# A fused linear-attention and SwiGLU block: all sixteen token tiles in Strassen pairs of the down projection, with the attention quotient inside its contraction

## Chip, cores and metric

One core of one Trainium2 chip. The metric is the device time of one execution in microseconds, the median of several runs. Engines: TensorE (PE) multiplies matrices, VectorE (DVE), ScalarE (ACT) and GpSimd (POOL) work on elements, SyncE (SP) issues transfers.

## The reference

The input x has 2048 tokens of 512 columns, bf16. It is normalised once, and two blocks read the result:

```python
xn = layernorm(x)
# A: linear attention, 32 heads of 16 columns
q, k, v = heads(xn @ wqkv)
pq, pk = phi(q), phi(k)              # phi(t) = (t + 1 if t > 0 else exp(t)) + 1e-6
kv, z = sum_s pk v^T, sum_s pk
o = (pq @ kv) / (pq . z + 1e-6)
# B: SwiGLU, 1792 hidden columns
h = silu(xn @ w_gate) * (xn @ w_up)
out = x + o @ wo + h @ w_down
```

## The kernel before

The kernel writes out its instructions by hand. Each call of `K.add` appends one entry to a list: an engine, its instructions, the keys that it reads (`r`) and writes (`w`), and older contents of the same memory (`a`). `number` turns the dependencies into semaphore waits. Every engine runs its entries in the order in which they were added; SP's transfers too go in that order. Tokens come in 16 tiles of 128.

*Phase one.* An order written out as one string (line 536 on) normalises the tiles, transposes them into `xnT`, and forms q and k (`proj`, L444, 512-column products). phi is made of an exponential on ACT (L465), a minimum on POOL (L472) and a sum on DVE (L483); phi(k) is `pk`, phi(q) is `pq`. `gacc` (L493) collects the products of xn with phi(k) in four PSUM banks, and `z_add` (L510, POOL) sums phi(k) over the tiles.

*Conventional gate and up products.* For the first three token tiles (`T0` = 384 columns), `gu` (L565) and `hop` (L613) make h for each of the 14 blocks of hidden columns. Beside them run the squares and maxima of the weights (L749, L756) for a power-of-two scale, kv (L625), its product M with wo (L711), the sum z over all partitions (L638), the weights' scaling by that power (`scale`, L849 and L850), and the x sums (L857) for the next stage.

*Strassen gate and up products.* The other 13 tiles make gate and up together in a Strassen-Winograd scheme: for each block `fc` and each half `q` of the tokens there are seven products of two 128-row steps (`prod`, L896, 416 columns), where a plain scheme has eight. ACT keeps and copies partial results between banks (`seed` L906, `keep5` L911) and forms silu (`gate0` L921, `gate1` L926); DVE combines PSUM with SBUF (`u4` L931, `up22` L936, `h21` L946); POOL makes the fourth quarter of h (`h22`, L940). DVE also sums the weights for two blocks ahead (`w_sums`, L857). `fill` puts single 512-column products of the down projection of tiles 0 to 3 (`ounits`: 14 of h with wd, L719, and four of the quotient with M, L723) between the Strassen products.

*The attention quotient.* For one tile after the other: POOL multiplies phi(q) by z into `pz` (L665), for six of the tiles folds it once (L674), DVE sums it over each head (`den_sum`, L678) and takes the reciprocal (L684), POOL multiplies phi(q) by that (`pq_mul`, L691), and SP transposes the result into a slot of `pk` (L697). `after` keys on `pq_mul` and `pz_mul` make POOL wait for a named sum of DVE.

*Down projection.* Tiles 4 to 15 go in six pairs through the same seven-product scheme, with seven steps of 128 hidden rows in each half. ACT copies and scales the pair's h (`hcopy`, L1076); DVE forms four sums of its quarters (`h_sum`, L1088, 128 x 896) and of wd's quarters (`t_sum`, L1039; `t1_part`, L1030); `dprod` (L1104) has seven 256-column products; `attn` (L1110) adds the quotient's part with four more products to each of the four outputs; ACT copies two partial results (L1116, L1120), DVE combines (`dkeep_y` L1124 and `du4` L1130, both from PSUM) and adds x (`dout`, L1136), and SP stores (L729).

```python
S_[0] = A21 + A22; S_[1] = S_[0] - A11
S_[2] = A11 - A21; S_[3] = A12 - S_[1]
```

are the four h sums of a pair, A11 and A12 the first and second half of the hidden columns of its first tile, A21 and A22 those of its second.

Of the kernel before, what the change touches and what calls it, by code (L numbers as in the profile page):

```python
# [9 lines left out]
P = 128  # L10
# [19 lines left out]
SX = -22  # L30
# [6 lines left out]
ORDER = tuple(range(14)) + (15, 14)  # L37
SLOT = {t: i for i, t in enumerate(ORDER)}
PAIRS = (4, 6, 8, 10, 12, 14)
H7 = 448  # L40
FOLD = range(3, 9)


class _Program:


# [6 lines left out]
    def add(self, eng, fns, r=(), w=(), dma=False, a=(), own=()):  # L53
# [11 lines left out]
        held = set().union(*[self.readers.get(k, set()) for k in own])  # L65
# [56 lines left out]
def bass_parallel_sum__linear_attn_block__swiglu_ffn__prompt_kernel(nc, A_x, A_wqkv, A_wo, B_x, B_w_gate, B_w_up, B_w_down, out):  # L122
# [5 lines left out]
    with contextlib.ExitStack() as es:  # L128
# [6 lines left out]
        xn = sb("xn", [P, NT, D], bf)  # L135
# [13 lines left out]
        pk = sb("pk", [P, NT, D], bf)  # L149
        pq = sb("pq", [P, NT, D], bf)  # L150
        hT = sb("hT", [P, 2, NFC, 512], bf)
# [12 lines left out]
        out_sb = sb("out_sb", [P, 2, D], bf)  # L164
# [27 lines left out]
        def tsum(ap):  # L192
# [15 lines left out]
        junks = [b_[:, :, :].rearrange("p a b -> p (a b)").bitcast(bf)[:, 0:F // 2] for b_ in (p5, c22)]  # L208
        xs = sb("xs", [P, 2, 2 * H7], f16)
        asd = sb("asd", [P, 8], f32)  # L210
        as1 = sb("as1", [P, 1], f32)
        as1b = sb("as1b", [P, 1], bf)
        sd = sb("sd", [P, 1], f32)
        ed = sb("ed", [P, 2], f32)
        idn = sb("idn", [P, 1], f32)
        sx = sb("sx", [P, 1], f32)
        iso = sb("iso", [P, 1], f32)
        sm = sb("sm", [P, 1], f32)
        psum = E(nc.psum_tensor("pb", [P, 8, 512], f32))
# [236 lines left out]
        def phi_exp(i, t):  # L456
            b = at[i, t]
            buf, bkey = ef[:, b - 4, :], ("ef", b - 4)
            if i == 0 and t in later:
                buf, bkey = pq[:, t, :], ("pq", t)  # L460
# [6 lines left out]
        def phi_min(i, t):  # L467
            buf, bkey = ef[:, at[i, t] - 4, :], ("ef", at[i, t] - 4)
            if i == 0 and t in later:
                buf, bkey = pq[:, t, :], ("pq", t)  # L470
# [5 lines left out]
        def phi_sum(i, t):  # L476
            b = at[i, t]
            dst, dkey = ((pk[:, t, :], ("pk", t)) if i else (pq[:, t, :], ("pq", t)))
            low, lkeys = (flo[:, t:t + 1], [("flo", t)]) if t in CENTRED else (1e-6, [])
            val, mid, keys = banks[b][:, :], ef[:, b - 4, :], [B(b), ("ef", b - 4)]  # L480
            if i == 0 and t in later:
                val, mid, keys = tq[later[t]], pq[:, t, :], [("tq", later[t]), ("pq", t)]
# [47 lines left out]
        def run(text):  # L530
            late = {int(w[1:]) for w in text.split() if w[0] == "z"}
            later.update({t: i for i, t in enumerate(int(w[1:]) for w in text.split() if w[0] == "u" and int(w[1:]) in late)})
            for w in text.split():
                steps[w[0]](int(w[1:]))

        run("""
            S0 M1 a0 b0 c0 R0 d0 F2 C1 S3 e0 N0 W1 r0 K0 o0 f0 R3 w1 S2 K1 P3 k0 S1 R2 J0 W3 x0 k1 Q1 L2 R1 w3
            m0 X2 q1 r1 Z2 Q3 s0 x1 o1 q3 S5 y1 K3 m1 k3 R5 n1 s1 G0 z1 L5 J1 x3 S9 K2 D5 Q0 z3 m3 S4 k2 R9 q0
            y3 P9 s3 G1 x2 S8 R4 m2 D9 Q2 z0 q2 P4 s2 R8 k5 z2 L8 n3 D4 S15 q5 x5 y0 S12 m5 G2 D8 y5 s5 q9 y2
            n5 S10 R15 k9 n0 y9 u5 R12 n9 k4 x9 L15 u9 D15 q4 m9 x4 L12 R10 s9 m4 q8 y4 D12 S11 P10 k8 z8 s4  # L540
            n4 R11 D10 G9 S13 x8 N11 A11 G5 m8 u4 y8 n2 s8 D11 G3 R13 S14 A0 P13 k15 S7 R14 k12 n8 D13 x15 L14
            S6 m15 q10 x12 D14 s15 m12 k10 y10 s12 n10 k11 x10 u10 R7 m10 q15 x11 s10 q11 m11 y15 L7 R6 s11
            D7 n15 k13 y11 u15 q13 n11 x13 L6 u11 D6 m13 q14 y13 s13 n13 q12 y14 u13 n14 k14 y12 u14 n12 q7
            x14 u12 m14 k7 y7 L1 s14 D0 D1 n7 k6 x7 u0 m7 q6 u7 x6 s7 m6 G4 y6 s6 n6 G12 u2 G14 u6 u1 G6 u8 G10
            u3 G11 G15 G8 G13 G7
        """)
# [11 lines left out]
        def gu(j, extra=(), er=(), ew=()):  # L558
            fc = j
            n = (len(extra) + 7) // 8  # L560
            todo = list(extra)
            for b, w_, key in ((gb(j), wg, "wg"), (gb(j) + 1, wu, "wu")):
                fns = []
                for c in range(NDC):
                    fns.append(lambda e, c=c, b=b, w_=w_: e.matmul(  # L565
                        banks[b][:, 0:T0], w_[:, c, fc * P:(fc + 1) * P], xnT[:, c, 0:T0],
# [794 lines left out]
```

## Time and profile before

| what | value |
|---|---|
| median of three runs | 199.56 us (199.41 to 199.59) |
| span of the profiled execution, first to last instruction | 198.2 us |
| what the median lies above that span | 1.4 us |
| TensorE's granted clock | 1.00 throughout |
| stage: Strassen gate and up products | 68.98 to 152.20 us |
| stage: down projection, to PE's end | 152.20 to 196.20 us |

The page gives the profiled execution's span; the time around it is taken from the median of the runs. How to read the profile's lines: in the table of engines, busy time, share of the span, number of instructions. In the groups: line, engine, operation, written and read tensors, shapes, count, then busy time and the mean of one in ns, then idle time of the engine before them and what ended it. In the timelines: start in us, length in us (of a run of several, if "x2" or more), engine, line, operation. In the view of one line: least, median and greatest length in ns. In the stretches: their length, then busy time of PE, weight loads, DVE, ACT, POOL with numbers of instructions, then clock and transfers.

### The profile page before, as it was taken

What the parts mean: (1) busy time and instruction counts of PE and PEld (TensorE: products, weight loads), DVE (VectorE), ACT (ScalarE), POOL (GpSimd) and SP (SyncE); (2) the same over time, 40 slices, a digit from 0 to 9 for tenths busy, and PEclk for the clock granted to TensorE, in tenths of its full rate; (3) what the DMA queues carried; (4) which work ended last, traced back from release to release, by engine and by line L of the source; (5) the groups of instructions that cost most, each with busy time, mean ns of one, the idle gap of its engine ahead of it and who ended that gap; (6) DMA issues with size and microseconds to landing.
All of it is one profiled execution on the core that took longest, in us unless ns stands there. A gap on an engine that the chain in (4) does not pass through costs nothing.

```text
span 198.2 us, 3561 instructions
## 1 busy us (share of the span) xinstructions
PE 193.8 (98%) x1193; PEld 115.2 (58%) x1207; DVE 170.6 (86%) x328; ACT 157.3 (79%) x314; POOL 127.6 (64%) x158
## 2 busy tenths in 40 slices
PE   8899999999999999999999999999999999999995
PEld 2344444444655555555555555555555888888884
DVE  2999998896997799887888998887888999998886
ACT  3799888699698998898999888998897967575300
POOL 3687877799999487689778877868579004413220
PEclk9999999999999999999999999999999999999999
DMA  5943248799900000111110221111000012132223
GB/s 171 360 131 81 61 86 231 211 275 373 348 14 0 3 0 0 28 26 30 28 26 2 55 53 26 26 26 31 2 0 2 3 40 66 33 77 66 45 65 121
DMA packets 28899, 15.97 MB, mean 81 GB/s; under 512 B 17232, under 2 KB 28880, under 8 KB 28880
## 3 DMA queue, kind: packets, MB, share of 16 engines
q1 hardware_dynamic: 28320, 15.28, 28.1%
q10 hardware_dynamic: 560, 0.46, 0.7%
q8 instruction: 9, 0.15, 0.3%
q14 instruction: 10, 0.08, 0.1%
HBM read 9.70 MB, written 2.10 MB: 60 GB/s over the span
## 4 chain that ended last, share of the span: by engine, by line
PE 94%; DVE 2%; DMA 2%; issue 1%; ACT 0%; POOL 0%; SPq 0%
PE pb L896 35%; PE pb L1104 16%; PE pb L444 13%; PE pb L565 9%; PE pb L493 7%; PE pb L719 6%; PE pb L1110 5%; DMA x_sb<-in_A_x_dram 2%; PE pb L723 2%; PE pb L625 0%; PE pb L711 0%; DVE pq L483 0%; PE pb L407 0%; POOL ef L472 0%; DVE stats L307 0%
## 5 line engine op out<-in xcount | busy, mean ns | idle before, releaser
L691 POOL TENSOR_TENSOR pq<-pq,rden 128x512 bf16<-128x512 bf16 x16 | 16.9, 1056 | 36.2 <-DVE rden L684 26.7
L896 PE MATMUL pb<-xnT,wgu 128*128 128x416 bf16 x112 | 26.6, 339 | 0.0
L444 PE MATMUL pb<-wqkv,xnT 128*128 128x512 bf16 x110 | 25.1, 379 | 0.2
L665 POOL TENSOR_TENSOR pz<-pq,zbc 128x512 f32<-128x512 bf16 x16 | 18.9, 1180 | 5.1 <-ACT pz L658 3.5
L565 PE MATMUL pb<-xnT,wgu 128*128 128x384 bf16 x112 | 19.9, 326 | 0.1
L931 DVE TENSOR_TENSOR pb<-p,pb 128x416 f32<-128x416 f32 x28 | 16.6, 595 | 3.6 <-PE pb L896 1.9
L472 POOL TENSOR_SCALAR ef<-ef 128x512 bf16<-128x512 bf16 x25 | 15.5, 620 | 5.8 <-ACT ef L465 5.6
L926 ACT ACTIVATE zacc<-pb,iw 128x416 bf16<-128x416 f32 x28 | 16.4, 614 | 3.1 <-PE pb L896 2.3
L444 PEld LDWEIGHTS pb<-wqkv,xnT 128*128 128x128 bf16 x112 | 10.9, 98 | 13.4 <-DVE pk L483 0.4
L936 DVE TENSOR_TENSOR c<-pb,p 128x416 f32<-128x416 f32 x28 | 16.4, 588 | 2.3 <-PE pb L896 0.3
L465 ACT ACTIVATE ef<-pb 128x512 bf16<-128x512 f32 x25 | 14.8, 593 | 3.9 <-PE pb L444 3.9
L940 POOL TENSOR_TENSOR hT<-c,zacc 128x416 bf16<-128x416 f32 x16 | 15.3, 974 | 2.3 <-ACT zacc L926 1.7
L510 POOL TENSOR_TENSOR zacc<-zacc,pk 128x512 f32<-128x512 f32 x13 | 16.0, 1232 | 1.0
L906 ACT ACTIVATE pb<-pb 128x416 f32<-128x416 f32 x28 | 13.7, 501 | 3.0 <-PE pb L896 1.9
L896 PEld LDWEIGHTS pb<-xnT,wgu 128*128 128x128 bf16 x112 | 10.9, 98 | 8.7
L921 ACT ACTIVATE zacc<-pb,iw 128x416 bf16<-128x416 f32 x28 | 15.7, 626 | 0.0
L565 PEld LDWEIGHTS pb<-xnT,wgu 128*128 128x128 bf16 x112 | 10.8, 98 | 7.0 <-DVE xn L613 0.2
L1104 PE MATMUL pb<-wgu,xnT 128*128 128x256 f16 (+1 forms) x112 | 14.9, 273 | 0.0
L896 PE MATMUL pb<-xnT,wqkv 128*128 128x416 bf16 x56 | 14.4, 339 | 0.3
L896 PE MATMUL pb<-wo,wqkv 128*128 128x416 f16 x56 | 14.4, 339 | 0.0
L896 PE MATMUL pb<-GT,wqkv 128*128 128x416 f16 x56 | 14.4, 339 | 0.0
L307 DVE BATCH_NORM_STATS2 stats<-x_sb 128x6 f32<-128x512 bf16 x16 | 10.8, 678 | 3.2 <-DMA x_sb<-in_A_x_dram 3.2
(202 smaller groups left out, 494.1 us busy)
## 6 DMA issues: line engine op xcount, KB each, us to landing
x_sb<-in_A_x_dram SPq DMA_DIRECT2D x14, 128.0 KB, 3.8
wgu<-in_B_w_gate_dram SPq DMA_DIRECT2D x2, 896.0 KB, 5.2
wgu<-in_B_w_up_dram SPq DMA_DIRECT2D x2, 896.0 KB, 8.0
wd<-in_B_w_down_dram SPq DMA_DIRECT2D x2, 896.0 KB, 13.1
out_dram<-out_sb SPq DMA_DIRECT2D x24, 64.0 KB, 1.6
wqkv<-in_A_wqkv_dram SPq DMA_DIRECT2D x3, 256.0 KB, 4.4
wqkv<-in_A_wqkv_dram SPq DMA_DIRECT2D x1, 512.0 KB, 6.3
wo<-in_A_wo_dram SPq DMA_DIRECT2D x1, 512.0 KB, 8.8
```

The costliest lines, as they stand in the source:

```text
L444: K.add("pe", [(lambda e, c=c: e.matmul(banks[b][:, :], src[:, c, t * P:(t + 1) * P], wqkv[:, c, col:col + D], start=(c == 0), stop=(c == ...
L472: K.add("pool", lambda e: e.tensor_scalar(out=buf, in0=buf, scalar1=top, scalar2=0.0, op0=ALU.min, op1=ALU.max), r=[bkey] + tkeys, w=[bkey])
L510: K.add("pool", lambda e: e.tensor_tensor(out=dst, in0=acc, in1=more, op=ALU.add), r=[key, mkey], w=[dkey])
L565: fns.append(lambda e, c=c, b=b, w_=w_: e.matmul(banks[b][:, 0:T0], w_[:, c, fc * P:(fc + 1) * P], xnT[:, c, 0:T0], start=(c == 0), stop=( ...
L665: K.add("pool", lambda e: e.tensor_tensor(out=halves(i), in0=two(pq[:, t, :]), in1=two(zbc[:, :]), op=ALU.mult), r=[("pq", t), ("zbc",)] + ...
L691: K.add("pool", lambda e: e.tensor_tensor(out=heads(pq[:, t, :]), in0=heads(pq[:, t, :]), in1=rden[:, i, :][:, :, None].broadcast_to([P, N ...
L896: K.add("pe", [(lambda e, c=c: e.matmul(banks[bank][:, 0:TS], L[i][:, c, :], R[i][:, c, ts], start=(start and c == 0), stop=(c == 1), skip ...
L921: K.add("act", lambda e: e.activation(sil4[:, q, :], bk(a), ACT.Silu, scale=iw[:, 0:1]), r=[B(a), ("iw",)], w=[("sil4", q)], a=[("zacc", 0 ...
L926: K.add("act", lambda e: e.activation(sil4[:, 2 + q, :], bk(d), ACT.Silu, scale=iw[:, 0:1]), r=[B(d), ("iw",)], w=[("sil4", 2 + q)], a=[(" ...
L931: K.add("dve", lambda e: e.tensor_tensor(out=bk(d), in0=p5[:, q, :], in1=bk(b), op=ALU.subtract), r=[B(b), ("p5", q)], w=[B(d)])
L936: K.add("dve", lambda e: e.tensor_tensor(out=c22[:, q, :], in0=bk(b), in1=p5[:, q, :], op=ALU.subtract), r=[B(b), ("p5", q)], w=[("c22", q)])
L1104: K.add("pe", [(lambda e, k=k: e.matmul(split(banks[b][:, 0:HD]), L[:, k, :], cut[:, :, k * P:(k + 1) * P], start=(start and k == 0), stop ...
```

## The change

Several things are changed together.

1. **All 16 tiles in pairs.** `PAIRS` has eight pairs of any two tiles. `ounits`, `oout`, `fill` and `attn` go, and with them the 512-column products between the Strassen products.
2. **The quotient inside the contraction.** The transposed quotient of a tile is stored as two more steps beside the seven of each half of h, and M's quarters as two more steps beside wd's. Each of the seven products of a pair has nine steps, each h sum 1152 columns instead of 896, and `tx` adds four sums of M's quarters. The transposition is split in two.
3. **Memory.** One tensor `big` holds h and the quotient, over what were xn, pk and phase one's buffers. phi(q) of tiles 2 to 15 is kept where x lay; x is loaded a second time after the tile's transposition (`xagain`, SP). h no longer is copied: `h21` scales while it writes, and `hscale` scales in place what `h21` doesn't write (tiles 0 to 2 and from half of tile 9 on).
4. **The quotient.** `pq_mul` multiplies pz, which already holds phi(q) z, by the reciprocal; M's rows are divided by z instead (`z_column`, `z_turn`, `m_evac`). The fold goes; the head sums are full width for all tiles.
5. **Engines.** Of the 32 h sums 14 go to POOL and 18 to DVE; of the 21 weight sums four go to POOL; of the weight scalings eight go to DVE, three to ACT and three to POOL; the five maxima on DVE become squares on ACT. `dkeep_y` reads p5 in SBUF instead of PSUM.
6. **Dependencies.** `add` keeps every same-engine dependency except PE's, and orders two engines that read one bank. The `after` keys go.
7. **Order.** Everything from phase one to the end stands in one string; weight loads are spread into phase one. The Strassen products' bank b alternates between blocks.

```diff
-PAIRS = (4, 6, 8, 10, 12, 14)
+PAIRS = ((0, 1), (3, 4), (5, 6), (7, 8), (2, 9), (10, 11), (12, 13), (14, 15))
...
+            if k[0] == "bank":
+                deps |= {d for d in self.readers.get(k, ()) if self.ops[d]["eng"] != eng}
...
-            if o["eng"] == eng and not o["dma"] and d not in held:
-                raw = any(self.last_w.get(k) == d for k in r)
-                if eng == "pe" or not (raw or dma):
-                    continue
+            if o["eng"] == eng == "pe":
+                continue
...
+        pq = _Tiles(stretch(PQ, 2) + [x_sb[:, t, :] for t in range(2, NT)])
+        pk = _Tiles(stretch(7 * S, 8) + stretch(S9 + 7 * S, 8))
...
             K.add("pool", lambda e: e.tensor_tensor(
-                out=heads(pq[:, t, :]), in0=heads(pq[:, t, :]),
-                in1=rden[:, i, :][:, :, None].broadcast_to([P, NH, DH]), op=ALU.mult),
-                r=[("pq", t), ("rden", i)] + list(after), w=[("pq", t)])
+                out=two(pq[:, t, :]), in0=halves(i),
+                in1=rden[:, i, :][:, :, None, None].broadcast_to([P, NH, 2, DH // 2]), op=ALU.mult),
+                r=[("pz", i), ("rden", i)], w=[pqk(t)])
...
         def turn(t):
+            for h in (0, 1):
+                K.add("sp", lambda e, h=h: e.dma_start_transpose(
+                    out=big9[:, h, 7:9, t * P:(t + 1) * P], in_=pq[:, t, h * HD:(h + 1) * HD]),
+                    r=[pqk(t)], w=[("qT", t, h)], ...
...
+            K.add("dve", lambda e: e.scalar_tensor_tensor(
+                out=hslot(fc, lo), in0=bk(b), scalar=sx[:, 0:1], in1=sil4[:, q, :], op0=ALU.mult, op1=ALU.mult),
...
+        def hscale(t, n, half, eng):
+            lo = t * P if t < C0 else max(t * P, T1)
+            v = big9[:, half, 0:7, lo:(t + n) * P]
+            sc, k = (sx[:, 1:2], ("sx1",)) if t < C0 else (sx[:, 0:1], ("sx",))
+            times(eng, v, v, sc, ...)
...
+        def h_sum(p, i, eng="dve"):
...
+            K.add(eng, lambda e: e.tensor_tensor(out=S_[i], in0=a, in1=b, op=op),
...
-        def dprod(p, i, b, start, ks=range(7)):
+        def dprod(p, i, b, start, ks=range(9)):
...
-                out=c22[:, r, 0:HD], in0=dk(d), scalar=iso[:, 0:1], in1=x_sb[:, t, HD:], op0=ALU.mult, op1=ALU.add),
+                out=c22[:, r, 0:HD], in0=p5[:, r, 0:HD], scalar=iso[:, 0:1], in1=x_sb[:, t, HD:], op0=ALU.mult, op1=ALU.add),
...
+        def xagain(t):
+            K.add("sp", lambda e: e.dma_start(x_sb[:, t, :], xin[t * P:(t + 1) * P, :]), w=[("x", t)],
+                  a=[("Sd", 2, i) for i in range(3) if ("x", t) in xo[i]], dma=True)
```

The new order is a string of some 1,120 words. `pr.fc.i.q` is product i of block fc and half q, `dp.p.i` product i of pair p, `hx.p.i.e` h sum i of pair p on engine e (a ACT, v DVE, p POOL), `ws` a weight sum, `sk` a weight scaling, `bc` a copy of a quarter of wd, `ta`, `tm`, `tx` sums of wd's and M's quarters, `hs` an h scaling, `hb` h22, `ha` h21, `uu` u4, `up` up22, `se` seed, `ke` keep5, `pz`, `ds`, `dr`, `pm`, `tr` the quotient's steps, `xr` a second load of x, `dk`, `dy`, `du`, `do` the steps of a pair's outputs, `tb` the load of silu's table (now among pair 5's steps, where it stood ahead of the conventional products, L991). Two pieces, from the end of the Strassen products to the second pair, and the last:

```
tm.2.0 ke.13.1 up.13.0 hx.0.3.v uu.13.1 dp.0.5 pz.13 tx.2 tm.2.1 dp.1.1 pr.13.4.0 tm.3.1 ha.13.0
hb.12.1 bc.21.1.a pr.13.3.1 pm.10 dp.0.6 hx.2.2.p xr.3 de.1 hs.9.1.0.v dk.0 hs.14.1.0.a sj.13.1
hb.13.0 pr.13.7.1 tx.3 up.13.1 dp.1.2 du.0 dp.0.2 pr.13.4.1 xr.4 tm.3.0 dp.0.7 xr.6 hb.13.1
hx.1.0.v hx.1.2.p pz.12 dp.1.5 xr.5 hx.1.1.v dp.1.6 tm.4.1 tx.4 tm.4.0 dp.0.3 dy.0 dk.1 du.1 dp.1.7
...
dp.7.5 dp.6.7 do.5.2 de.7 hx.7.2.p dp.6.3 dy.6 dk.7 dp.7.6 do.6.3 hx.7.3.v do.6.1 dp.6.4 du.7
do.6.2 dy.7 do.6.0 dp.7.3 dp.7.7 do.7.3 dp.7.2 dp.7.4 do.7.1 do.7.0 do.7.2
```

More of the change, by code (lines that the diff above doesn't have):

```diff
@@ L528, in bass_parallel_sum__linear_attn_block__swiglu_ffn__prompt_kernel @@
         }
[L530 to L545, printed above, removed]
@@ new lines, in gu, with gu_kv, gate_conv @@
+                K.add("pe", fns, r=sum([xkeys(t) for t in range(C0)], []) + [(key, fc // 7) for fc in CONV[j]] +
+                      [(key + "c", fc) for fc in CONV[j]] + list(er), w=[B(b)] + list(ew))
+        def gu_kv(j):
+            gu(j, 0, kv_fns(), [("GT", c) for c in range(NDC)] + [("wqkv", 2, 0)], [B(0)])
+        def gate_conv(j):
+            K.add("act", lambda e: e.activation(sil[:, j % 2, 0:TW], banks[gb(j)][:, 0:TW], ACT.Silu),
+                  r=[B(gb(j))], w=[("sil", j % 2)])
@@ L618, in gt_evac, with hjk @@
+        def hjk(fc, lo, n):
+            return [("hj", fc, b) for b in range((lo - T0) // TS, (lo + n - 1 - T0) // TS + 1)]
         def gt_evac(c, eng):
@@ L766, in gather, with top_square @@
+        def top_square(k):
+            tops = [i for i in range(NN) if NORM[k][i][3] == "top"]
+            col = asum[:, NN * k + tops[0]:NN * k + tops[-1] + 1]
+            K.add("act", lambda e: e.activation(col, col, ACT.Square), r=[("asum", k, i) for i in tops], w=[("asum", k, i) for i in tops])
         def gather():
@@ L1326, in bass_parallel_sum__linear_attn_block__swiglu_ffn__prompt_kernel @@
+        """)
+        K.add("sp", [], r=[("out", t, c) for t in range(NT) for c in (0, HD)])
         K.number()
```

881 lines of the change are left out of this document (361 added, 520 removed).

## The prediction

> **What bounds the kernel now.** I read the page's table of engines and its chain first, then the busy time by stage, then the chain in order of time.
>
> ```profile
> span 198.2 us, 3561 instructions
> PE 193.8 (98%) x1193; PEld 115.2 (58%) x1207; DVE 170.6 (86%) x328; ACT 157.3 (79%) x314; POOL 127.6 (64%) x158
> PE 94%; DVE 2%; DMA 2%; issue 1%; ACT 0%; POOL 0%; SPq 0%
> ```
>
> PE is on the chain for 94% of the span and busy for 98%. The busy time by stage (columns: PE, weight loads, DVE, ACT, POOL) shows how near the others are. The four stretches are the end of phase one, the conventional gate and up products (prep), the Strassen gate and up products (U), and the down projection (D):
>
> ```profile
> 40.10:48.74 8.64, 8.59 (x42) 3.91 (x41) 6.82 (x8) 8.54 (x16) 8.07 (x8) 1.00 1.01 322
> 48.74:68.98 20.24, 20.09 (x133) 12.24 (x134) 17.28 (x32) 17.56 (x40) 16.73 (x14) 1.00 0.32 104
> 68.98:152.20 83.22, 82.86 (x455) 44.25 (x460) 72.08 (x137) 76.23 (x147) 64.78 (x65) 1.00 0.10 21
> 152.20:196.20 44.00, 43.88 (x395) 38.13 (x394) 39.64 (x79) 24.03 (x33) 9.68 (x10) 1.00 0.20 53
> ```
>
> In U, DVE works 72.1 and ACT 76.2 of 83.2 us, with POOL at 64.8; in D, POOL is nearly idle. So the bound is PE, but only while its stage stays as long as it is. The chain in order of time prices PE's work, start and length in us:
>
> ```profile
> 144.39 0.65 PE pb L719 x3
> 145.04 3.52 PE pb L896 x20
> ...
> 156.64 3.06 PE pb L1104 x28
> ...
> 160.90 0.44 PE pb L1110 x4
> ...
> 196.17 0.48 DVE out_sb L1136
> ```
>
> A 512-column product costs 0.217 us, a 416-column one 0.176, a 256-column one 0.1093 (L1104) or 0.110 (L1110).
>
> **What the change does to PE.** It removes 4 x 14 products of L719 and 4 x 4 of L723 (72 x 0.217 = 15.6), 6 x 7 x 7 of L1104 (294 x 0.1093 = 32.1) and 12 x 8 of L1110 (96 x 0.110 = 10.6): 58.3 us. It adds 8 pairs x 7 products x 9 steps, 504 x 0.1093 = 55.1, and some 0.2 for the z column. Net: -3.0 us. Against the profiled execution that is 198.2 - 3.0 = 195.2 of span; the median of the runs stands 1.4 above the span, so 196.6 is the time if PE stays the bound. But the 72 removed 512-column products were PE's filler: 83.2 - 14 x 28 x 0.176 = 14.2 us, some 66 of them, ran between the Strassen products of U. U shrinks from 83.2 us to 14 x 28 x 0.176 = 69.0 plus six interleaved down products of 9 x 0.1093, 5.9, and 0.8 of others: 75.7 us. DVE, ACT and POOL have much the same work to do in it.
>
> **What the change does to POOL and DVE.** Two views must be read together: the timelines of DVE and of POOL at the same moment. First, a sum of two SBUF tiles on DVE that starts during a POOL instruction:
>
> ```profile
> 189.15 1.06 POOL L691 TENSOR_TENSOR pq<-pq,rden 128x512 bf16<-128x512 bf16 x1 [3.24 <-DVE rden L684]
> ```
> ```profile
> 189.29 1.40 DVE L1088 TENSOR_TENSOR xnT<-GT 128x896 f16<-128x896 bf16 x1
> ```
> ```profile
> L1088 DVE TENSOR_TENSOR xnT<-GT x3: 609/615/1398, 161.8 to 189.3; 128x896 f16<-128x896 bf16 x3
> ```
>
> It takes 1.40 us for 0.61: POOL ends at 190.21, DVE at 190.69, 0.48 us later. So it waits until POOL is done and then needs 0.48, its 0.61 less 0.13 of start. The other way round, and with an f32 input:
>
> ```profile
> 70.21 1.39 POOL L665 TENSOR_TENSOR pz<-pq,zbc 128x512 f32<-128x512 bf16 x1 [0.85 <-ACT pz L658]
> 71.58 2.98 POOL L850 TENSOR_SCALAR wgu<-wgu,sw 128x1024 bf16<-128x1024 bf16 x2
> ```
> ```profile
> L850 POOL TENSOR_SCALAR wgu<-wgu,sw x3: 1114/1887/1889, 63.6 to 73.4; 128x1024 bf16<-128x1024 bf16 x3
> ```
> ```profile
> L857 DVE TENSOR_TENSOR wqkv<-xnT,GT x1: 1868/1868/1868, 70.6 to 70.6; 128x1664 f16<-128x1664 bf16 x1
> ```
> ```profile
> 41.89 0.68 DVE L483 SCALAR_TENSOR_TENSOR pq<-pb,ef 128x512 bf16<-128x512 f32 x1
> 42.49 0.73 DVE L483 SCALAR_TENSOR_TENSOR pq<-hT,flo,pq 128x512 bf16<-128x512 f32 x1
> 43.16 2.77 DVE L483 SCALAR_TENSOR_TENSOR pq<-hT,pq 128x512 bf16<-128x512 f32 x2
> ```
>
> Here a DVE x sum begins at 70.6 inside POOL's L665, ends late at 72.5, and POOL's scaling of 71.58, behind it, takes 1.89 instead of 1.11. Two DVE sums of two SBUF tiles took 2.77 at 43.16, where one of the same kind took 0.73 at 42.49. DVE instructions that read PSUM show nothing of it (this one ran inside a POOL instruction that began at 163.86 and took 1.06):
>
> ```profile
> 164.54 0.43 DVE L1130 TENSOR_TENSOR pb<-pb,p 128x256 f32<-128x256 f32 x1 [0.28 <-PE pb L1104]
> ```
>
> So POOL's instructions and those of DVE that read only SBUF (two inputs, or one scaled) exclude each other. I call their summed time the **pair's** time; it can't be less than the stage.
>
> [...]
>
> The prices:
>
> ```profile
> L665 POOL TENSOR_TENSOR pz<-pq,zbc 128x512 f32<-128x512 bf16 x16 | 18.9, 1180 | 5.1 <-ACT pz L658 3.5 <-DVE xn L1088 1.6
> L691 POOL TENSOR_TENSOR pq<-pq,rden 128x512 bf16<-128x512 bf16 x16 | 16.9, 1056 | 36.2 <-DVE rden L684 26.7 <-DVE wqkv L857 8.6 <-DVE as L802 0.8
> L940 POOL TENSOR_TENSOR hT<-c,zacc 128x416 bf16<-128x416 f32 x16 | 15.3, 974 | 2.3 <-ACT zacc L926 1.7 <-DVE c L936 0.5
> L1018 POOL TENSOR_SCALAR wgu<-wd,sd 128x896 bf16<-128x896 bf16 x4 | 4.0, 1012 | 3.5 <-DVE mixb L1030 3.5
> L674 POOL TENSOR_TENSOR pz<-pz 128x256 f32<-128x256 f32 x6 | 4.0, 667 | 0.5
> L510 POOL TENSOR_TENSOR zacc<-zacc,pk x13: 1151/1157/1818, 45.5 to 61.3; 128x512 f32<-128x512 f32 x13
> L857 DVE TENSOR_TENSOR wqkv<-wgu x7: 680/680/970, 66.7 to 134.6; 128x1024 f16<-128x1024 bf16 x7
> L857 DVE TENSOR_TENSOR wqkv<-wqkv,wgu x7: 415/417/472, 67.4 to 140.4; 128x512 f16<-128x512 f16 x7
> ```
>
> The order puts 14 of the 32 h sums on POOL, 1152 columns each. No row has that. Two-input POOL instructions run from 667 ns at 256 columns to 1157 at 512, 1.91 ns a column, whatever their types: 0.67 + 896 x 1.91 ns = 2.38 us. The low bound is the one-input L1018: 1.012 x 1152/896 = 1.30; the high one is L940's rate, 2.70. I take 2.38, as L665, L510, L674 and L940 lie on that line and L1018 has one input.
>
> POOL from the end of the projections (40.1) on: 15 z adds and two scalings 19.7; 16 pz 18.9; 16 quotients, now from f32 pz, between 1.06 and 1.18, at 1.1: 17.6; 28 h22 27.3; 14 h sums 33.3; four weight sums 5.4; three weight scalings 3.3; five h scalings 5.1; two wd copies 2.0; half of M 1.1; the last two minima 1.2. Together 134.9; neighbours' records overlap by about 0.04, so 130.5. DVE's SBUF-only instructions, each less 0.13: 18 h sums of 0.61 (0.615 + 256 x 0.51 ns - 0.13; 0.51 is (680 - 417)/512 from L857) 11.0; 17 weight sums 6.5; four x sums 3.5; eight weight scalings now on DVE 2.6; T parts and T sums 5.1; four M sums 1.2; h and wd scalings 1.3; eight dkeep_y, which now read p5 instead of PSUM, 2.8. Together 34.0. The pair needs **164.5 us** after 40.1; before it was 99.3 (the four POOL shares above) + some 25 = 124 of 156. PE has 156.1 - 3.0 = 153.1 there.
>
> The last h sum is followed by four products of 0.98 (3.9 us), the last output sum (0.48) and its store (1.6). So 40.1 + 164.5 + 6.0 + 1.4 outside the span = 212.0 if the pair never idles. In 40.10:48.74, with ready work queued, POOL was busy 93%; at 93% the pair takes 177 and the time is 224.5. I take 98%, nearer full since DVE fills POOL's gaps: 167.9 and, rounded, **215.5 us**.
>
> **Edits costed at nothing, and what covers them.** `add` now keeps every same-engine dependency off PE, and orders readers of a bank on two engines: an added wait costs DVE the 0.08 by which records overlap, only between direct neighbours; below 2 us in all, hidden unless DVE is the bound. What queues behind it on DVE are PSUM sums that PE waits for. Removed hcopies (ACT) and top squares: ACT is not the bound in D. The split transposes and the second loads of x go on SP's queue:
>
> ```profile
> L697 SPq DMA_TRANSPOSE pk<-pq x16: 1189/1196/1197, 78.9 to 190.2; - x16
> x_sb<-in_A_x_dram SPq DMA_DIRECT2D x14, 128.0 KB, 3.8
> out_dram<-out_sb SPq DMA_DIRECT2D x24, 64.0 KB, 1.6
> ```
>
> 32 half transposes at 0.6 to 1.2 us take SP 19 to 38 us of 150 and 14 loads at about 0.5 another 7, so stores are not held up for long. Each x load lands in 3.8 us and is issued eight or more products (7.9 us) ahead of its dkeep_y: hidden, at most 4 us if the last were late. The weight loads move ahead of transposes in phase one; one transpose behind 896 KB could be late by some 4 us, with three projections queued before its reader: nothing. The load of silu's table is written at pair 5 now, though silu is used from the conventional products on:
>
> ```profile
> L991 ACT ACT_TABLE_LOAD x1 | 1.3, 1283 | 0.0
> ```
>
> one more load of 1.3 us on ACT at most, in prep or in D, where ACT has room (17.6 of 20.2 and 24.0 of 44.0): nothing, 1.3 without that cover.
>
> **The rivals.** (a) *PE stays the bound*: the sums fall into POOL's gaps, 196.6, faster. It would need the pair's demand under 153; against it stands 164.5. Even without exclusion U's 75.7 us would be nearly full: DVE's 72.1 loses two x sums and two output adds and gains six weight scalings, full-width head sums and the first h, T and M sums, an estimate of 75; ACT's 76.2 loses ten weight scalings (11.5) and gains the norms and evacuations of M and more of wd's norms and copies, an estimate of 73. (b) *Sums of 16-bit tiles on POOL are cheap*: at 1.30 the pair loses 14 x 1.08 = 15.1, demand 149.4, and near-full DVE and ACT cost a few per cent of U: 199 to 205. For it: no row has two 16-bit inputs of one step. [...] (c) *DVE, in order, becomes the bound*: each of its 35 SBUF-only instructions in U waits on average half a POOL instruction, 0.55, so 19 on top of 75: 94 for 75.7; in D 31 x 0.7 on 39: 61 for 49.5. 196.6 + 18 + 11.5 = 226.
>
> **How the numbers follow.** Forecast 0.58 (207 to 224: 2.16 us per POOL sum and start-ups that overlap, to the pair at 93%); (a) 0.12; (b) 0.13; (c) 0.17. The range reaches from 201, the middle of (b), to 226. What a measurement tells from no change is 0.2%, 0.4 us. Faster: (a) and the luckiest part of (b), 0.13; same 0.02; slower 0.85.
>
> **What would show it.** L1088's successor on POOL at 2.2 to 2.5 us (1.3 speaks for b); DVE's h and weight sums late by hundreds of ns whenever a POOL instruction is under way; PE busy under 93% with the chain passing through POOL and DVE in U and early D; PE idle before products that read a DVE result. PE at 98% and a chain of PE alone would prove the pair wrong; ACT or SPq on the chain would mean a cause that I have not priced.

## The result and the profile after

| | before | after |
|---|---|---|
| median | 199.49 us (199.09 to 199.59) | 235.51 us (234.43 to 236.89) |
| ratio, 95% interval | | 1.182 (1.177 to 1.187) |
| span of the profiled execution | 198.2 us | 232.8 us |

The change costs 36 us, where the forecast said 16. In this table and those below, executions that fell in a second, slower state (one of e2, 231.7 us, and one of e4, 207.8 us) are left out of medians and ranges. The page after, with the table of engines:

```profile
PE 203.8 (88%) x1248; PEld 119.2 (51%) x1253; DVE 195.9 (84%) x341; ACT 145.8 (63%) x288; POOL 177.2 (76%) x172
```

PE no longer fills the span: 29 us of it are idle, where before 4.4 were. The chain that ended last stops after 1% of the span at a wait that the profile does not show, so the stretches have to tell where the time went (PE, weight loads, DVE, ACT, POOL, then the granted clock). They are a part of phase one, U, D to PE's end, and the last part of D:

```profile
30.00:40.00 10.00, 7.95 (x28) 3.10 (x30) 5.04 (x9) 4.36 (x11) 3.83 (x7) 0.83 1.15 319
...
76.93:164.03 87.10, 79.63 (x455) 41.33 (x452) 86.06 (x152) 72.35 (x144) 80.86 (x68) 1.00 0.09 21
164.03:230.52 66.49, 55.29 (x450) 45.77 (x450) 49.11 (x77) 15.21 (x24) 38.58 (x19) 0.92 0.24 64
...
210.00:232.80 22.80, 17.40 (x144) 14.77 (x144) 13.53 (x24) 1.50 (x4) 3.79 (x2) 0.93 0.23 64
```

The same part of phase one before:

```profile
30.00:40.00 10.00, 9.95 (x47) 4.55 (x47) 8.91 (x17) 7.49 (x16) 7.18 (x13) 1.00 0.79 223
```

Three different things show. In phase one every engine works less than before, PE does 28 products for 47, and the DMA share is higher. In U DVE is busy 86.1 of 87.1 us and PE is not. In D no engine is full: something makes them wait for each other.

**Phase one.** The timeline of SP (start, length, line, operation), and PE at the same time:

```profile
25.87 0.58 SPq L247 DMA_DIRECT2D wgu<-in_B_w_gate_dram  x1
26.49 1.19 SPq L443 DMA_TRANSPOSE xnT<-big  x1
27.73 0.58 SPq L247 DMA_DIRECT2D wd<-in_B_w_down_dram  x1
28.36 5.13 SPq L443 DMA_TRANSPOSE xnT<-big  x3
```
```profile
31.96 12.37 PE L464 MATMUL pb<-wqkv,xnT 128*128 128x512 bf16 x47 [2.48 <-DMA xnT<-big]
```

The transposes stand behind large weight loads. From issue to landing they take a median of 3.7 us after, and 2.5 before:

```profile
xnT<-big SPq DMA_TRANSPOSE x14, 3.7
```
```profile
xnT<-xn SPq DMA_TRANSPOSE x14, 2.5
```

**U and early D.** POOL's h sums cost what was forecast, but DVE's sums beside them are late. POOL first, then DVE:

```profile
L1020 POOL TENSOR_TENSOR xnT<-big 128x1152 f16<-128x1152 bf16 x6 | 15.0, 2505 | 6.4 <-PE pb L1038 6.4
```
```profile
156.51 2.54 POOL L1020 TENSOR_TENSOR wqkv<-big 128x1152 f16<-128x1152 bf16 x1
...
163.50 2.74 POOL L1020 TENSOR_TENSOR xnT<-big 128x1152 f16<-128x1152 bf16 x1
...
174.72 2.87 POOL L1020 TENSOR_TENSOR xnT<-big 128x1152 f16<-128x1152 bf16 x1
```
```profile
156.76 2.77 DVE L962 TENSOR_TENSOR wgu<-wgu,mixb 128x896 f16<-128x896 bf16 x1
...
163.95 2.91 DVE L1020 TENSOR_TENSOR xnT<-big 128x1152 f16<-128x1152 bf16 x1
...
168.42 0.61 DVE L962 TENSOR_TENSOR wgu<-wgu 128x896 f16<-128x896 bf16 x1
...
170.56 0.47 DVE L1053 SCALAR_TENSOR_TENSOR c<-p,iso,x_sb 128x256 f32<-128x256 f32 x1
...
175.93 1.95 DVE L1053 SCALAR_TENSOR_TENSOR c<-p,iso,x_sb 128x256 f32<-128x256 f32 x1
...
178.59 0.74 DVE L1020 TENSOR_TENSOR GT<-ef,big 128x1152 f16<-128x1152 f16 x1
```

Read each long DVE line against POOL's: the T sum of 156.76 began inside POOL's sum of 156.51 and took 2.77 us for 0.61; the h sum of 163.95 took 2.91 for 0.74; the dkeep_y of 175.93, 1.95 for 0.47.

**D.** From the waits (us in total, times, longest), and from SP's timeline:

```profile
PE pb L1038 <- DVE pb L1059: 4.9, 1, 4.9
```
```profile
200.55 5.04 SPq L678 DMA_TRANSPOSE big<-x_sb  x4
205.63 1.05 SPq L1063 DMA_DIRECT2D out_dram<-outx  x2
```

PE stands 4.9 us once for DVE's `du4` (L1059), and four transposes in a row keep SP for 5 us, with stores of finished outputs behind them. Which of these things costs how much is for the experiments.

### The profile page after: what moved, and what is told of

It reads as the page before. It is cut to its first block, busy times and chain, and to the rows that moved or that the text cites. A ratio compares the mean times of both kernels' runs of the same rounds, so it can differ in the third digit from the quotient of the medians.

```text
span 232.8 us, 3689 instructions
## 1 busy us (share of the span) xinstructions
PE 203.8 (88%) x1248; PEld 119.2 (51%) x1253; DVE 195.9 (84%) x341; ACT 145.8 (63%) x288; POOL 177.2 (76%) x172
## 5 line engine op out<-in xcount | busy, mean ns | idle before, releaser
L907 POOL TENSOR_TENSOR big<-c,zacc 128x416 bf16<-128x416 f32 x28 | 30.6, 1102 | 5.2 <-DVE c L898 3.8
L1038 PE MATMUL pb<-wgu,big 128*128 128x256 bf16 (+1 forms) x184 | 24.0, 276 | 3.4 <-DVE outx L1069 2.9
L1045 ACT ACTIVATE pb<-pb 128x256 f32<-128x256 f32 x8 | 3.0, 370 | 34.3 <-DVE outx L1069 31.4
L1038 PEld LDWEIGHTS pb<-wgu,big 128*128 128x128 bf16 x184 | 17.8, 99 | 6.8 <-DVE outx L1069 3.5
L485 ACT ACTIVATE ef<-pb 128x512 bf16<-128x512 f32 x25 | 14.8, 593 | 9.4 <-PE pb L464 9.3
L1020 POOL TENSOR_TENSOR xnT<-big 128x1152 f16<-128x1152 bf16 x6 | 15.0, 2505 | 6.4 <-PE pb L1038 6.4
L671 POOL TENSOR_TENSOR x_sb<-pz,rden 128x512 bf16<-128x512 f32 x14 | 17.7, 1265 | 2.4 <-DVE rden L667 2.4
L530 POOL TENSOR_TENSOR zacc<-zacc,big 128x512 f32<-128x512 f32 x13 | 18.1, 1392 | 0.9
L655 POOL TENSOR_TENSOR pz<-x_sb,zbc 128x512 f32<-128x512 bf16 x14 | 18.0, 1288 | 0.6
L913 DVE SCALAR_TENSOR_TENSOR big<-pb,sx,zacc 128x416 bf16<-128x416 f32 x28 | 17.6, 641 | 0.5 <-PE pb L865 0.5
L879 ACT ACTIVATE p<-pb 128x416 f32<-128x416 f32 x28 | 14.2, 516 | 2.5 <-DVE c L898 1.1
```

Source lines behind the costliest of these rows:

```text
L530: K.add("pool", lambda e: e.tensor_tensor(out=dst, in0=acc, in1=more, op=ALU.add), r=[key, mkey], w=[dkey])
L655: K.add("pool", lambda e: e.tensor_tensor(out=halves(i), in0=two(pq[:, t, :]), in1=two(zbc[:, :]), op=ALU.mult), r=[pqk(t), ("zbc",)], w=[ ...
L671: K.add("pool", lambda e: e.tensor_tensor(out=two(pq[:, t, :]), in0=halves(i), in1=rden[:, i, :][:, :, None, None].broadcast_to([P, NH, 2, ...
L907: K.add("pool", lambda e: e.tensor_tensor(out=hslot(fc, lo), in0=c22[:, q, :], in1=sil4[:, 2 + q, :], op=ALU.mult), r=[("c22", q), ("sil4" ...
L913: K.add("dve", lambda e: e.scalar_tensor_tensor(out=hslot(fc, lo), in0=bk(b), scalar=sx[:, 0:1], in1=sil4[:, q, :], op0=ALU.mult, op1=ALU. ...
L1038: K.add("pe", [(lambda e, k=k: e.matmul(split(banks[b][:, 0:HD]) if k < 7 else banks[b][:, 0:HD], L[:, k, :], cut[:, :, k * P:(k + 1) * P] ...
```

## The experiments

The theories: **A**, the pair (POOL, and DVE's instructions that read only SBUF) is the bound, as forecast; **B**, weight loads ahead of phase one's transposes; **C**, SP's order in D (second loads of x and stores behind transposes); and rival (c) of the forecast, DVE in order, which became **Y** (its own added work) and **X** (its lateness beside POOL). Every version's time stands beside the kernel before in the same set of runs (199.2 to 199.6).

### h sums back on DVE, and late loads

e1 gives the 14 h sums of POOL to DVE at their places (the first of pair 0 moved to directly ahead of the second); e2 issues six weight loads after the last transpose of phase one; e3 does both; e4 puts ten h sums of the kernel before on POOL.

```diff
 # e1, in the order
-hx.2.2.p ... hx.7.2.p
+hx.2.2.v ... hx.7.2.v
 # e2, in the order
-... N0 W1 ld.3 r0 ...
+... N0 W1 r0 ...
-... L1 s14 D0 D1 n7 ...
+... L1 s14 D0 D1 ld.0 ld.1 ld.2 ld.3 ld.4 ld.5 n7 ...
 # e4, in the kernel before, h_sum
-K.add("dve", ...
+K.add("pool" if p and i in (0, 2) else "dve", ...
```

> The changed kernel with the 14 h sums that stood on POOL given to DVE, at the same places of the order (the first of pair 0 directly ahead of the second); nothing else differs. Theory A (POOL and DVE's SBUF-only instructions exclude each other, and their summed time is the bound from phase one's end on): the pair loses 14 x (2.36 - 0.61) = 24.5 us, the time falls by 18 to 25 us, to 210 to 218. Rival (each engine's own work is the bound; DVE was busy 196 of 233 us and gets 14 x 0.74 = 10.4 more): no faster, 235 to 246.

> The changed kernel with its six weight loads taken out of phase one and issued after phase one's last transposition, in the order of the kernel before; all else as changed. Theory B (the weight loads ahead of transpositions hold phase one up: the last projection ended at 46.1 us instead of 40.1): 6 to 8 us faster, 227 to 230. Rival (the time is given back, since the pair of POOL and DVE bounds what follows and the norms then wait for the weights): 0 to 3 us faster, 232 to 236.

> Both edits: h sums all on DVE and the weight loads after phase one. If A and B are separate costs they add: 202 to 211 us. If they share a cause (both only shift the same wait): no better than the better one alone by more than 2 us.

> The kernel before with one part of the change alone: the first and third h sum of pairs 1 to 5 of the down projection on POOL (10 sums of 896 columns), the other 14 on DVE. Theory A: each takes 0.67 + 640 x 1.91 ns = 1.89 us on POOL, and DVE's sums of the stage wait for them; DVE's outputs queue behind: 3 to 10 us slower than before, 203 to 210. Rival (no exclusion that matters, engines bound by their own work): DVE loses 10 x 0.53 us, POOL rises from 10 to 29 of 44 us: unchanged, 198.5 to 200.

| version | median, us | ratio to before |
|---|---|---|
| e1, h sums on DVE | 228.40 (226.26 to 229.38) | 1.144 (1.137 to 1.150) |
| e2, late loads | 227.71 (226.76 to 227.83) | 1.140 (1.136 to 1.144) |
| e3, both | 220.93 (220.82 to 221.40) | 1.109 (1.106 to 1.112) |
| e4, before with ten POOL sums | 205.30 (204.32 to 205.97) | 1.029 (1.024 to 1.034) |

e2 confirms B with 7.8 us. In its trace, with the same columns as above, phase one is full again and a transpose lands in a median of 2.6 us:

```profile
30.00:40.00 10.00, 9.95 (x47) 4.52 (x47) 9.09 (x16) 7.85 (x18) 7.29 (x12) 1.00 0.84 224
```
```profile
xnT<-big SPq DMA_TRANSPOSE x14, 2.6
```

e4 shows that POOL sums alone make the kernel before slower, by 5.9 us for ten sums. The one execution with a profile, that of 207.8 us, shows the path there. POOL, DVE and PE:

```profile
158.16 2.15 POOL L1088 TENSOR_TENSOR xnT<-GT,ef 128x896 f16<-128x896 bf16 x1 [4.79 <-ACT ef L1076]
160.28 2.25 POOL L1088 TENSOR_TENSOR xnT<-GT 128x896 f16<-128x896 bf16 x1
```
```profile
158.50 4.51 DVE L1039 TENSOR_TENSOR wgu<-wgu 128x896 f16<-128x896 bf16 x2
```
```profile
163.46 1.67 PE L1104 MATMUL pb<-wgu,xn 128*128 128x256 f16 x7 [3.15 <-DVE out_sb L1136]
```

Two T sums on DVE take 4.51 us beside two h sums on POOL, where one took 0.62 in the kernel before. An output sum stands behind them in DVE's order, and PE waits 3.15 us for that. PE's listed waits in D are all for DVE, none for a POOL sum itself.

e1 met neither expectation: giving the sums back brings 7.1 us, far less than the 18 that theory A asked for. The two gains add (14.6 together), but 21.5 us stay. Theory A as a bound falls here: without the POOL sums the pair's demand, by the forecast's own prices, is 164.5 - 33.3 + 14 x 0.61 = 139.7 us, below PE's 153.1. Yet e3 does not become bound by PE (stretches of e3, as above):

```profile
100.00:110.00 10.00, 10.00 (x57) 4.98 (x56) 9.78 (x21) 9.94 (x21) 9.92 (x10) 1.00 0.13 26
...
140.00:150.00 10.00, 7.65 (x49) 4.12 (x47) 10.00 (x16) 6.62 (x13) 5.86 (x6) 1.00 0.01 3
```

From 100 us all four engines are full at once; from 140 us DVE alone is, and PE waits for it.

### What fills DVE, and what it waits for

All four start from e3. e5 and e6 leave out one half each of the quotient of tiles 2 to 9, e7 moves two loads, e8 moves DVE's weight scalings.

```diff
 # e5, in the order
-pz.3 pm.3 pz.4 pm.4 ...   (tiles 2 to 9)
 # e6, in the order
-ds.3 dr.3 ds.4 dr.4 ...   (tiles 2 to 9)
 # e7, in the order
-... xr.2 ... tr.10 ... xr.7 ... tr.11 ... tr.13 ... xr.8 ...
+... xr.2 xr.7 xr.8 ... tr.10 ... tr.11 ... tr.13 ...
 # e8, in the order (eight words)
-sk.0.1.v sk.0.4.v ...
+sk.0.1.a sk.0.4.a ...
```

> The version with the h sums on DVE and the late loads, without POOL's two quotient multiplications for tiles 2 to 9 (so phi(q) of these tiles goes into the contraction undivided); 16 POOL instructions of 1.18 us go from the gate/up Strassen stage, DVE's instructions all stay. In that version (220.9 us) DVE's instructions of this stage last 94.1 us in sum, of which 83.6 are their undisturbed durations and 10.5 lateness beside POOL. Theory X, the lateness is what is left to explain: POOL's busy time in the stage falls from 65 to 46 us, so about 3 of the 10.5 us go and more by the waits that they hand on: 215 to 218 us. Theory Y, DVE's own added instructions: 220 to 221.5 us.

> The same version without DVE's row sum and reciprocal of the denominators of tiles 2 to 9 (these tiles are divided by those of tiles 0 and 1); 8 x (0.71 + 0.35) = 8.5 us of DVE's own work go from the gate/up Strassen stage, POOL's instructions all stay. Theory Y, DVE in its order is the bound there and its own work (83.6 us against 75.0 in the kernel before) is the excess: 6 to 9 us less, 212 to 215 us, at most to where ACT's own 79.5 us of the stage bind. Theory X, only the waits beside POOL count: 219.5 to 221.5 us.

> The same version with the second loads of x for tiles 7 and 8 issued on SP ahead of the first transposes of the D stage instead of behind three of them. In its trace DVE stood 4.2 us at the sum that takes tile 8's x, whose load SP issued at 182.5 us behind four transposes, and behind DVE's wait stood the reciprocals for which POOL's quotients, and behind these the next transposes, waited 12.9 us. Theory C, this loop through SP's order is what D loses: 4 to 7 us less, 214 to 217 us. Rival, the transposes are late by DVE's load alone and another wait takes its place: 219.5 to 221.5 us.

> The same version with DVE's eight weight scalings of 0.71 us given to ACT, where such a piece takes 1.15 us, as it did in the kernel before. Theory Y with X: DVE loses 5.7 us of its own work in the gate/up stages and about 2.8 us of lateness beside POOL: 4 to 8 us less, 213 to 217 us. Rival, ACT with 79.5 us of its own in an 84 us stage is full as well and takes DVE's place: 220 to 226 us.

| version | median, us | against e3 |
|---|---|---|
| e5, no POOL multiplications | 218.64 (218.37 to 219.38) | -2.3 |
| e6, no denominators on DVE | 220.83 (220.29 to 221.22) | -0.1 |
| e7, x early | 217.13 (216.76 to 217.31) | -3.8 |
| e8, scalings on ACT | 223.04 (222.85 to 223.29) | +2.1 |

e5 lies between its two expectations, nearer to X. e6 refutes Y in this form: 8.5 us less work on DVE, and no gain. Two stretches of e6, against those of e3 above, say why. From 100 us DVE falls from 9.78 to 8.25, but PE was full there already, with 57 products, and ACT and POOL stay at 9.94 and 9.92. From 140 us, where DVE alone is full, these denominators are long done and DVE stays at 10.00. So e6 does not test DVE where it binds.

```profile
100.00:110.00 10.00, 10.00 (x57) 4.92 (x56) 8.25 (x15) 9.94 (x21) 9.92 (x10) 1.00 0.13 27
...
140.00:150.00 10.00, 7.66 (x48) 4.10 (x47) 10.00 (x16) 6.61 (x13) 5.78 (x5) 1.00 0.01 2
```

e8 shows the other side. At 80 to 90 us DVE is idle for over a third, and ACT is full:

```profile
80.00:90.00 10.00, 8.00 (x44) 3.68 (x41) 6.12 (x13) 10.00 (x20) 5.82 (x6) 1.00 0.13 26
```

e7 fell just short of the 4 us that C asked for, but its mechanism is in the lines of e3. DVE, SP and POOL in e3:

```profile
179.92 0.71 DVE L661 TENSOR_REDUCE den<-pz 128x32 f32<-128x544 f32 x1
184.83 0.48 DVE L1053 SCALAR_TENSOR_TENSOR c<-p,iso,x_sb 128x256 f32<-128x256 f32 x1 [4.20 <-DMA x_sb<-in_A_x_dram]
...
186.29 0.34 DVE L667 RECIPROCAL rden<-den 128x32 f32<-128x32 f32 x1
```
```profile
175.89 5.98 SPq L678 DMA_TRANSPOSE big<-x_sb  x4
...
182.54 0.43 SPq L1077 DMA_DIRECT2D x_sb<-in_A_x_dram  x1
```
```profile
186.71 1.44 POOL L671 TENSOR_TENSOR x_sb<-pz,rden 128x512 bf16<-128x512 f32 x1 [12.85 <-DVE rden L667]
```

It is a loop through three queues, each in order. SP issues x behind four transposes; DVE stands 4.2 us for x; behind DVE's wait stands the reciprocal; POOL waits for that, and the next transpose for POOL.

### Leaving the elementwise work out

All four start from e7. e9 leaves out the 14 h sums, e10 the whole quotient of tiles 2 to 15, e11 both; e12 is complete and gives ACT eight late scalings.

```diff
 # e9, in the order (the 14 words that POOL had)
-hx.0.0.v hx.0.2.v hx.2.2.v ...
 # e10, in the order
-pz.2 ds.2 dr.2 pm.2 ...   (tiles 2 to 15)
 # e12, in the order (eight words)
-bc.22.0.v hs.9.1.0.v hs.9.1.1.v hs.11.1.1.v hs.10.1.1.v ms.0.p hs.11.1.0.p bc.21.0.p
+bc.22.0.a hs.9.1.0.a hs.9.1.1.a hs.11.1.1.a hs.10.1.1.a ms.0.a hs.11.1.0.a bc.21.0.a
```

> The version with DVE's h sums, late loads and early x (217.1 us), without the 14 h sums that the change had given to POOL: their products use what lies in the buffers. DVE loses 14 x 0.75 = 10.5 us of its own and some 3 us of lateness, all from 138 us on, where DVE is busy 9.7 to 10.0 of every 10 us until 170 and 8 to 8.6 after. Theory, DVE in its order is the bound from there on: 206 to 211 us. Rival, the quotients' loop (DVE's reciprocal, POOL's multiplication, SP's transposes) sets the pace of the D stage: 214 to 217.5 us.

> The same version with all h sums, without the attention quotient of tiles 2 to 15: no floor products, row sums, reciprocals and divisions (14 each of POOL's two multiplications of 1.18 us and of DVE's 0.71 and 0.35 us), so phi(q) goes into the contraction as it is. DVE loses 14.8 us, POOL 33 us, and SP's transposes wait for nobody. Leaving out either half alone moved the time by -2.3 and -0.1 us. Theory, DVE and POOL bind in turn, so both must go: 207 to 212 us. Rival, the quotients lie beside other work altogether: 214 to 217.5 us.

> The same version without these 14 h sums and without the quotient of tiles 2 to 15. Theory, the elementwise work of DVE and POOL is the whole excess over TensorE's own instructions (196.6 us by the forecast): 199 to 204 us. Rival, the added waits within an engine, SP's order or the second loads of x hold a part that no elementwise work explains: 206 to 212 us.

> The complete version with DVE's h sums, late loads and early x, and eight late scalings (of h and of the down projection's weights; five of DVE's, three of POOL's) given to ACT, which is busy 6.5 of 10 us at 140 to 150 us and under 3.5 of 10 thereafter. DVE loses about 2 us of its own from 136 us on and 2 to 3 us of lateness beside POOL's pieces. Theory, DVE is the bound from 120 to 170 us: 212 to 215 us. Rival, ACT's copies and seeds come late behind the scalings: 216.5 to 219 us.

| version | median, us | against e7 |
|---|---|---|
| e9, no 14 h sums | 215.01 (213.28 to 215.55) | -2.1 |
| e10, no quotient | 208.51 (207.86 to 209.05) | -8.6 |
| e11, neither | 208.54 (207.82 to 209.12) | -8.6 |
| e12, late scalings on ACT | 216.61 (216.53 to 216.75) | -0.5 |

The quotient is the larger part: its two halves bring 2.3 and 0.1 alone in tiles 2 to 9, and the whole of tiles 2 to 15 brings 8.6. Whether the six further tiles make this difference, or both halves going together, was not tried. The 14 h sums, once on DVE, bring 2.1, and nothing on top of the quotient.

e9 and e12 met their rivals. In e9 PE does get faster where DVE binds (the stretch below, 7.65 in e7), but most of it is lost again at 190 us, where PE waits 3.5 us for `du4`:

```profile
140.00:150.00 10.00, 9.39 (x61) 5.41 (x59) 10.00 (x17) 8.19 (x16) 7.03 (x6) 1.00 0.06 16
```
```profile
PE pb L1038 <- DVE pb L1059: 3.5, 1, 3.5
```

e11 met its rival too: 9.3 us over the kernel before stay with neither kind of work. Its SP, DVE and PE show one cause, the same wait:

```profile
177.42 5.05 SPq L678 DMA_TRANSPOSE big<-x_sb  x4
182.51 1.91 SPq L1063 DMA_DIRECT2D out_dram<-outx  x2
```
```profile
178.12 0.49 DVE L1069 SCALAR_TENSOR_TENSOR outx<-pb,iso,x_sb 128x256 bf16<-128x256 f32 x1 [0.16 <-DMA out_dram<-outx]
...
185.69 0.48 DVE L1069 SCALAR_TENSOR_TENSOR outx<-pb,iso,x_sb 128x256 bf16<-128x256 f32 x1 [5.46 <-PE pb L1038]
```
```profile
187.91 0.94 PE L1038 MATMUL pb<-wgu,xnT 128*128 128x256 bf16 x7 [3.03 <-DVE pb L1059]
...
188.91 1.48 PE L1038 MATMUL pb<-mixb,ef 128*128 128x256 f16 x7
```

The output sum of 178.12 is done at 178.6, but SP is issuing transposes and sends its store, the second of the two from 182.51, only at 183.99. The next sum into the same buffer, at 185.69, waited for that store, which by estimate landed at 185.6: 183.99 and the 1.6 us that output stores took from issue to landing (the median after, in e2 and in e3); the 5.46 us of idle time before it are put down to PE, whose products for it were long done. Behind that sum stands `du4`, and behind that PE.

### Stores on another queue

e13 starts from e7, e14 from e11, e15 from e12; in all three ACT issues the stores.

```diff
 # in store
-            K.add("sp", lambda e: e.dma_start(oview[t * P:(t + 1) * P, lo:hi], out_sb[:, s_, lo:hi]),
+            K.add("act", lambda e: e.dma_start(oview[t * P:(t + 1) * P, lo:hi], out_sb[:, s_, lo:hi]),
```

> The complete version with DVE's h sums, late loads and early x (217.1 us), with the 32 stores of the output issued by ACT instead of SP. In its trace a store was issued up to 4.4 us after its sum, behind four transposes that take SP 5 us to issue, but no sum waited over 0.2 us for its output buffer before 210 us. Theory, DVE and the quotients hold the D stage and SP's stores lie beside them: 215.5 to 217.5 us. Rival, SP's order is what is left: 211 to 214.5 us.

> The version without the 14 h sums and without the quotient of tiles 2 to 15 (208.5 us), with the stores issued by ACT. In its trace the sum of pair 4's first quarter is done at 178.6 us, SP issues its store at 184.0 us behind four transposes (177.4 to 182.5 us), the next sum into that buffer starts at 185.7 us, TensorE stands 3.0 us until 187.9 us, and its granted clock is 0.87 from 190 to 200 us. Theory, SP's order is what is left over TensorE's own instructions in the D stage: 4 to 5.5 us less, 203 to 204.5 us. Rival, other waits take its place: 207 to 208.5 us.

> The complete version with everything that helped: DVE's h sums, late loads, early x, the eight late scalings on ACT (216.6 us) and the stores issued by ACT. As it stands no theory lets it beat the kernel before: if SP's stores lie beside DVE's work, 215 to 217 us; if SP's order is what is left, 210 to 214 us.

| version | median, us | against its start |
|---|---|---|
| e13, e7 with ACT's stores | 219.88 (219.25 to 220.07) | +2.7 |
| e14, e11 with ACT's stores | 205.36 (205.13 to 205.88) | -3.2 |
| e15, e12 with ACT's stores | 218.53 (218.10 to 218.89) | +1.9 |

In e14 the stall is gone and PE is full from 170 to 200 us, though the gain is under the 4 us that the expectation had as its least:

```profile
180.00:190.00 10.00, 10.00 (x94) 8.96 (x93) 5.44 (x11) 2.89 (x6) 0.00 (x0) 1.00 0.12 34
```

In the complete kernel the same edit costs 2.7 us (1.9 in e15), which neither theory had. Its ACT shows that the wait has only changed its queue:

```profile
187.58 1.96 ACTq L1063 DMA_DIRECT2D out_dram<-outx  x3
189.59 0.38 ACT L1049 ACTIVATE p<-pb 128x256 f32<-128x256 f32 x1 [5.10 <-DVE outx L1069]
```

ACT, in order, stands at a store for DVE's late output sum, and its next copy of PE's result (`dkeep`, L1049) comes behind that, after 5.1 us without work. `du4` waits 0.83 us for this copy, and PE 1.90 us for the h sum behind `du4`. No version beats the kernel before; the best complete one is e12, with 216.6 us.

## Why the prediction was wrong

The direction was right, and the forecast's mechanism is there, but it is one term of several and not the bound. In the forecast's sum, 40.1 + 167.9 + 6.0 + 1.4, phase one's 40.1 became 46.1, and the rest of the profiled span, 173.9, became 186.7. These are 18.8 of the 20 us that were missed; the rest lies outside that span. Going from the kernel after to the kernel before by the steps above:

| term | us | shown by |
|---|---|---|
| weight loads ahead of phase one's transposes | 7.8 | after to e2 |
| 14 h sums on POOL rather than DVE | 6.8 | e2 to e3 |
| second loads of x behind transposes | 3.8 | e3 to e7 |
| the attention quotient of tiles 2 to 15 | 8.6 | e7 to e10 |
| the 14 h sums on DVE, with the quotient gone | 0.0 | e10 to e11 |
| stores behind transposes | 3.2 | e11 to e14 |
| rest | 5.9 | e14 to before |

The steps depend on their order, as e9 and e13 show; the sum is the 36 us. The kernel before has a quotient and h sums too, so those rows aren't work that the change added: they are what such work costs where it no longer lies beside a PE that is busy anyway. e14 still takes 5.9 us more than the kernel before, with less elementwise work.

**"One transpose ... late by some 4 us, with three projections queued before its reader: nothing."** This step failed first, by 7.8 us. The weight loads made the transposes slow (a median of 3.7 us for 2.6), several in a row, so no queue of three projections could hide them, and PE's clock fell on top (0.83).

**The pair at 98% as the bound.** The price of a POOL sum was right: 2.38 forecast, 2.36 the median of six, 2.50 their mean, with the longest at 2.87. The exclusion was right too: two of DVE's sums took 2.77 us for 0.61 and 2.91 for 0.74 beside POOL, and a scaling of DVE with one input (L805, at 77.99 after) 1.25 for 0.71, ending 0.29 us after POOL. What failed was the step from it to a bound: the pair's summed time was taken as what one must wait for, and the pair as never idle. But from 210 us on POOL works 3.8 and DVE 13.5 of 22.8 us, so the pair is idle for 5.5 us at least there. And DVE works in order, so a sum that waits for POOL holds the PSUM sums behind it, for which PE waits (3.15 us in e4's rows), and that counts in DVE's time and not in the pair's. With the POOL sums gone the pair fell to about 140 us, and the time went to 220.9 and not to 196.6 (e3).

**Rival (c)** named the right engine and gave 226. U came out at 87.1 us, with DVE busy for 86.1, where (c) had 94; D came out at 66.5, where it had 61; phase one's 6 us were in neither. But DVE isn't a bound that a few us less work move: e6 took 8.5 us away for nothing, e8 5.7 for a loss, e10 14.8 from DVE and 33 from POOL for 8.6.

The expectation of e5 adds up DVE's durations in e3's U to 94.1, the forecast's 94, but this is chance: 83.6 and 10.5 of lateness there, 75 and 19 in the forecast. Records of neighbours also overlap (by 0.08 us at 42.49 in the prediction's rows of DVE), so such a sum is more than busy time. For the same reason the 83.6 and ACT's 79.5 in e6's expectation can't be set against PE's 75.7. In busy time the estimates under rival (a), 75 for DVE and 73 for ACT, were near: ACT is busy 72.4 us of U, and DVE in e3 84.7, less 10.5 an estimate of 74. What was too low is U's length of 75.7. Without the quotient and 14 h sums DVE, ACT and POOL are busy for 71.6, 71.5 and 47.6 us, and U still takes 79.6 (e14, the stage ahead of U and U):

```profile
40.45:71.31 30.86, 28.73 (x173) 15.27 (x171) 25.59 (x41) 26.70 (x40) 29.09 (x23) 1.00 0.53 163
71.31:150.95 79.64, 77.92 (x456) 42.80 (x454) 71.61 (x132) 71.54 (x144) 47.63 (x44) 1.00 0.09 21
```

**"So stores are not held up for long"**, and second loads of x "hidden, at most 4 us if the last were late". The bound was right (3.8, e7), the choice of nothing wrong. Summing SP's time (19 to 38 of 150 us) hid the order: four transposes come in a row, 5 to 6 us, and what stands behind them is late by all of it. For the stores 3.2 us are shown only where the quotient and the sums are left out (e14); in the complete kernel what they cost could not be seen apart, since ACT's queue was no better place (e13).

**PE's -3.0 us.** The engine table of e14 stands at

```profile
PE 194.6 (95%) x1253; PEld 118.2 (58%) x1253; DVE 165.7 (81%) x313; ACT 145.3 (71%) x288; POOL 106.5 (52%) x130
```

Against 193.8 before, PE is busy 0.8 us longer, not 3.0 shorter. How much of these 3.8 us is a wrong price stays open, as no run shows it apart; in U it is 77.9 for 75.7. Of e14's 5.9 us over the kernel before, these 0.8 and 9.4 - 4.4 = 5.0 of idle PE time (span less busy) are the two parts. Of the latter, 3.3 lie in the two stages above: PE idles 2.1 and 1.7 us there, and 0.2 and 0.4 in the prediction's lines of before. What it waits for there no run took apart; the added waits within an engine, which the prediction put below 2 us, are a candidate.

**What held:** the price of h sums on POOL, late DVE sums beside POOL, PE under 93%, idle before products that read a DVE result. That sums on DVE and on POOL aren't free beside each other is shown by the rows of 156.76 and 163.95 us (2.77 for 0.61, 2.91 for 0.74), and by e4, where ten sums alone cost 5.9 us.

## What to carry to other kernels

Where the other engines are nearly as busy as the bound, as here in U (DVE 72 and ACT 76 of 83 us), shortening the bound's work leaves them no room: take each engine's busy time in the new stage, with its lateness, before counting on the gain. Moving work between them need not cure it (e8, e12), and an experiment that takes work away says something only of the stretch in which that work lay (e6). Where two engines exclude each other, as DVE's SBUF sums and POOL here (2.77 us for 0.61), price the wait in the order of the engine that waits, since everything queued behind it waits as well (PE 3.15 us in e4). A queue is judged by its longest run of slow issues, here four transposes of 5 to 6 us together, and by what stands behind that, never by its total.

## What the runs showed of the hardware

**PE's granted clock fell after some pauses**, which the prediction had not considered. The kernel before had 1.00 throughout. In e11, after the 3.03 us of the row at 187.91, seven 256-column products took 1.48 us, where those of 187.91 took 0.94, and the stretch has a clock of 0.87:

```profile
190.00:200.00 10.00, 10.00 (x82) 8.48 (x81) 4.82 (x10) 1.13 (x3) 0.00 (x0) 0.87 0.25 72
```

With 82 products for the 94 of the ten us from 170 in the same run, the pause of 3 us cost more than itself. No simple limit follows: in the kernel after a pause of 2.48 us in phase one was followed by 0.83, while e3, whose clock was 1.00 throughout, had this one:

```profile
PE pb L1038 <- DVE GT L1020: 2.6, 1, 2.6
```

**DVE's wait for POOL isn't confined to sums of two 16-bit tiles.** `dkeep_y`, with one f32 tile from p5 and one from x, took 1.95 us for 0.47 at 175.93, and ended 0.29 us after the POOL sum that was under way (174.72 to 177.59).
